# Fourier filter and gated convolution on one core: the last two blocks' convolution done block by block, the first spectral rows loaded ahead of constants, and the whole order laid out again

## The chip, the core and the metric

The kernel runs on one core of a Trainium2 chip. The metric is device time in microseconds (us). Before the change the median of three runs was 847.21 us (846.08 to 847.69). The engines are named as the profile names them: PE multiplies matrices (PEld is its weight load), DVE and ACT work element by element, POOL and SP here mostly issue transfers. Each engine executes its own instructions strictly in the order in which the program lists them.

## What is computed

```python
# x: (8, 3200, 256) float32; w_r, w_i: (256, 256); b_r, b_i: (256)
X = np.fft.rfft(x, axis=1)
Yr = Xr @ w_r - Xi @ w_i + b_r
Yi = Xr @ w_i + Xi @ w_r + b_i
Yr, Yi = soft_threshold(Yr, 0.01), soft_threshold(Yi, 0.01)   # shrink by 0.01 towards 0
y = np.fft.irfft(Yr + 1j * Yi, n=3200, axis=1)

# y then goes through a gated convolution, kernel size 5, causal, one filter per channel
gate = 1 / (1 + np.exp(-sum(conv_w[k] * y_shifted_by(4 - k) for k in range(5))))
val = y @ w_val
out = (gate * val) @ w_out
```

`w_val`, `conv_w` and `w_out` can reach the kernel as 64-bit floats; it turns them into 32-bit ones with integer operations on DVE.

## The kernel before

Eight sequences (index b) are processed in a software pipeline. A transform of length 3200 = 64 x 50 is done in two steps each way, as matrix products:

- **p1** (`p1`, unit u = 0..7): load rows of x, multiply with a 50-point transform (PE, tile `p`, L716 to L723), copy half of the result to SBUF with ACT (tile `s`, L729), form sums and differences with DVE (L736), and store to an intermediate array in device memory, `a_dram` (the stores are issued at L671 and L751, half of them by SP and half by POOL). x has 3 buffers and s has 2 for sequences 1 to 7. Sequence 0 borrows further buffers, since nothing else runs yet.
- **p2** (block d = 0..6): when all of a sequence's `a_dram` is stored, load 4 x 128 rows of it (tile `a`, issued by SP at L771, two transfers), do the second transform step (`s2`, L789), split the result into a high and a low part (ACT L830, L834, L841; DVE L837, L838, L842, tiles `sx` and `xs`), multiply with the complex weights (`mix_sum` L907 and `mix` L903, tile `y_ps`), soft-threshold (ACT L915, DVE L917, tile `tp`), do the first inverse step (`s1i`, L858) and store to `z_dram`. There are 13 units of mixing per sequence (`NU`), the unit of time of the order.
- **p3** (block k = 0..7): load from `z_dram` (tile `zl`), do the last inverse step (`positions`, L969, tile `y_p`), copy to `y_sb`. The convolution (`conv`) takes two blocks k and k+1 at a time: one ACT multiply of 800 columns for each of the two channel halves (L1017), four DVE multiply-adds of 800 columns for each half (L1020), one ACT sigmoid for each half (L1030). Then, for each block (`gated`): the product with `w_val` (tile `v_ps`), gate times value (DVE L1054), a cast and its rest (ACT L505, DVE L507) and the product with `w_out` (tile `o_ps`, L1003), a copy (L1079) and the store. The last two blocks of sequence 7 skip the cast and use plain 32-bit weights (L999).

**The order.** Every piece of work is entered with `add(at, engine, ...)`, where `at` is its due time in units of mixing. `Plan.order` is a list scheduler with a cost for each piece and modelled transfer landings. Whenever an engine is free it takes, of the pieces that could begin within 20 ns of the earliest one (50 ns on SP), the one with the lowest `at`. The result is the fixed instruction order of each engine. On the chip the engines wait for semaphores. A piece that is listed ahead of its data therefore holds up all that stands behind it on that engine. The dictionary `O` holds the offsets of `at` for each kind of piece, some of them for each sequence (`conv_6`), and a few switches: `together` and `hold` decide how readily PE pieces of the modes "q" and "h" (the small transform products) are grouped, `early_x` says for how many of sequence 0's last stores the first x loads of sequence 1 need not wait. Where PE would stand idle in the model between 4 us and 200 us, `fill` puts products with zeros (L480) there, whose result is not used.

In sequence 0 the first `a` load has `at` = 0 + `load_a` + `load_a_0` = 10.0 + 3.6 = 13.6, while the constants that also become ready when sequence 0's stores have landed have -90.4 (`load_g1`, L607, part 0) and about 0 and 4 (`load_f2`, L602, parts 1 and 2).

Of the kernel before, what the change touches and what calls it, by code (L numbers as in the profile page):

```python
# [21 lines left out]
NH = 2  # L22
# [275 lines left out]
def act(n, kind="copy"):  # L298
# [9 lines left out]
O = {'spread': -101.4442,  # L308
     'hold': 1.6848,
     'together': 1.5823,  # L310
     'later': 53.134,
     'load_x': 17.846,
     'p1': 1.5226,
     'p1_step': 1.0759,
     'load_a': 10.0019,
     's2': -2.121,
     's1i': -11.205,
     'p3': 7.122,
     'load_z': 9.4509,
     'y': 9.4717,  # L320
     'conv': 47.943,
     'val': 3.9688,
     'gate': -49.7775,
     'project': 6.045,
     'late_val': 6.023,
     'late_out': 14.484,
     'turn': -90.4451,
     'pre': -5.7976,
     'mix_sum': -1.2289,
     'p1_1': -9.8046,  # L330
     'load_x_1': -91.0314,
     'p1_2': -1.912,
     'p3_0': -0.0087,
     'cast': 0.0037,
     'cast_sum': 24.9973,
     'store': -14.2917,
     'store_1': 42.1645,
     'load_a_0': 3.5715,
     'lag': 5,
     'early_x': 4,  # L340
# [3 lines left out]
     'const': 1.7737,  # L344
     'load_x_0': 6.2588,
     'load_x_2': 11.2939,
     'load_x_3': 1.4455,
     'load_x_6': -5.698,
     'load_x_7': -13.6801,
     'store_0': 2.4949,  # L350
     'store_2': -3.9049,
     'store_3': 5.6479,
     'store_6': 7.9572,
     'store_7': -7.113,
     'load_a_1': -10.8481,
     'load_a_2': 3.8573,
     'load_a_3': -7.0617,
     'load_a_6': 3.0623,
     'load_a_7': -2.8157,
     's2_0': -0.1117,  # L360
     's2_1': 0.2815,
     's2_2': -0.0057,
     's2_3': 0.3165,
     's2_6': -0.036,
     's2_7': 0.9309,
     's1i_0': -16.6791,
     's1i_1': 0.7475,
     's1i_2': 0.3771,
     's1i_3': -9.836,
     's1i_6': -9.5474,  # L370
     's1i_7': 2.8801,
     'mix_sum_0': -0.2547,
     'mix_sum_1': -0.1504,
     'mix_sum_2': -0.9431,
     'mix_sum_3': 0.2288,
     'mix_sum_6': -0.0331,
     'mix_sum_7': 0.5012,
     'cast_0': 0.1408,
     'cast_1': 1.6748,
     'cast_2': 0.1173,  # L380
     'cast_3': -1.1395,
     'cast_6': 0.0469,
     'cast_7': 0.8641,
     'load_z_0': -2.2847,
     'load_z_1': 12.2789,
     'load_z_2': 6.4162,
     'load_z_3': 0.5923,
     'load_z_6': 9.1799,
     'load_z_7': -17.648,
     'y_0': -2.4138,  # L390
     'y_1': 7.1844,
     'y_2': -0.27,
     'y_3': 9.8876,
     'y_6': -17.7978,
     'y_7': -0.7363,
     'val_0': 0.0788,
     'val_1': 0.0095,
     'val_2': 0.5223,
     'val_3': -0.3875,
     'val_6': 1.5935,  # L400
     'val_7': -0.1154,
     'gate_0': 1.29,
     'gate_1': -6.6514,
     'gate_2': 10.3642,
     'gate_3': -13.7452,
     'gate_6': 6.0847,
     'gate_7': 5.6435,
     'project_0': -0.2308,
     'project_1': -0.2082,
     'project_2': 0.3489,  # L410
     'project_3': -0.0372,
     'project_6': 1.4085,
     'project_7': 0.8587,
     'conv_0': -12.5894,
     'conv_1': 3.8899,
     'conv_2': -5.0339,
     'conv_3': -7.0043,
     'conv_6': -5.8596,
     'conv_7': 8.2268,
     'pre_0': 6.5561,  # L420
     'pre_1': -14.0279,
     'pre_2': 4.4971,
     'pre_3': 10.0304,
     'pre_6': 2.6289,
     'pre_7': 17.1354,
     'p1_0': 24.5364,
     'p1_3': 0.2909,
     'p1_6': 0.0365,
     'p1_7': 0.0276,
     'p3_1': 0.2371,  # L430
     'p3_2': -0.3606,
     'p3_3': 0.0793,
     'p3_6': -0.8783,
     'p3_7': 0.4373}
# [9 lines left out]
def fourier_filter_then_gated_conv(ctx: ExitStack, tc: tile.TileContext, x, w_r, w_i, b_r, b_i,  # L444
# [242 lines left out]
    def p1(b, u, at):  # L687
# [64 lines left out]
        for k, (eng, queue, cost) in enumerate(QUEUES[:1] * 2 if early and u > 4 else QUEUES):  # L752
            key = ("a_dram", b, 2 * u + k)
            A_KEYS.setdefault(b, []).append(key)
            if early:
                STORED.append(("stored", 0, 2 * u + k))
            add(at + of("store", b) + 0.001 * k, eng, cost * 1.7 if u == 0 else cost, lambda k=k, queue=queue: store(k, queue), [ks + (0,), ks + (1,)],
                [key] + ([STORED[-1]] if early else []), {ka: "a_dram"} if u == k == 0 else None, kb=200, chain="a" + eng, dmas=3 if u == 0 else 2, read=False)


    def p2(b, d, at):
# [10 lines left out]
        add(at + of("load_a", b), "SP", 1330, load, A_KEYS[b], [ka + (0,)], {ka: "a"}, kb=128 * nt, chain="a", dmas=2)  # L772
# [167 lines left out]
    def y_at(k, c, tap=H0):  # L940
        return y_of(k, tap)[:, c]
# [64 lines left out]
    def conv(b, kk, at):  # L1006
# [12 lines left out]
        def tap(c, j):  # L1019
            nc.vector.scalar_tensor_tensor(out=acc(c), in0=wide(c, j), scalar=cw_sb[:, c, j:j + 1], in1=acc(c), op0=ALU.mult, op1=ALU.add)  # L1020
        for c in range(2):
# [7 lines left out]
        for c in range(2):  # L1029
            add(at + of("conv", b) + 0.15, "ACT", act(2 * TB, "sigmoid"), lambda c=c: nc.scalar.activation(  # L1030
                out=acc(c), in_=acc(c), func=AF.Sigmoid), (), [kg + (c, e) for e in range(2)])

# [166 lines left out]
```

## Time and profile before

| what | value |
|---|---|
| median of three runs | 847.21 us (846.08 to 847.69) |
| profiled execution, its own time | 845.59 us |
| its span, first to last instruction | 843.8 us |
| mean granted PE clock | 0.993 |
| PE busy / DVE busy / ACT busy / POOL busy | 825.3 / 735.9 / 596.3 / 147.9 us |
| bytes moved | 162.33 MB, mean 192 GB/s |

The 1.79 us between the profiled execution's time and its span lie around the first and the last instruction. Busy PE time includes the products with zeros. In the views that follow, a row of a timeline gives the start in us, the length in us, engine, line, operation, output and inputs, the number of instructions merged into the row, and in brackets the idle time before it with what ended it. A row of the chain gives start, length, and what held the end at that moment. In the table by windows each engine's busy time is followed by its number of instructions, then come the granted PE clock, the transfer engines' busy share and the rate.

### The profile page before, as it was taken

How to read it: one execution, taken by the hardware profiler on the slowest of the kernel's cores; microseconds unless marked ns; L12 is line 12 of the kernel's file. 1: busy time of each engine (PE TensorE's matmuls, PEld its weight loads, DVE VectorE, ACT ScalarE, POOL GpSimd, SP SyncE). 2: the span in 40 equal slices, each digit the busy share in tenths (PEclk: the TensorE clock that was granted, in tenths of full speed). 3: DMA queues.
4: the chain of work that ended last, by engine and by line, in shares of the span. 5: the costliest groups of instructions: out<-in, count | busy, mean ns of one | idle time of the engine just before them, and what ended most of it. 6: DMA issues, size and time to landing. Idle time of an engine off the chain costs nothing.

```text
span 843.8 us, 24474 instructions
## 1 busy us (share of the span) xinstructions
PE 825.3 (98%) x10036; PEld 715.3 (85%) x10036; DVE 735.9 (87%) x1006; ACT 596.3 (71%) x903; POOL 147.9 (18%) x284
## 2 busy tenths in 40 slices
PE   9999989999999999999999999999999999999997
PEld 5777768888889889898989988898888899999775
DVE  3367796989988999989988999889989899979994
ACT  2246566787877787778787777778775778777662
POOL 5332222201221121302211031301212000000000
PEclk9899999999999999999999999999999999999999
DMA  8898999867877786767966696758875455336313
GB/s 191 246 238 229 266 230 271 224 173 223 241 187 199 204 225 193 196 171 219 266 204 173 180 251 194 222 144 217 249 211 157 136 154 161 108 100 172 109 64 98
DMA packets 122665, 162.33 MB, mean 192 GB/s; under 512 B 16496, under 2 KB 102266, under 8 KB 122554
## 3 DMA queue, kind: packets, MB, share of 16 engines
q1 hardware_dynamic: 109706, 134.73, 57.1%
q0 software_dynamic: 12848, 26.04, 12.0%
q8 instruction: 80, 1.31, 0.7%
q14 instruction: 31, 0.25, 0.1%
HBM read 82.06 MB, written 78.64 MB: 190 GB/s over the span
## 4 chain that ended last, share of the span: by engine, by line
PE 75%; DVE 14%; DMA 6%; ACT 2%; issue 2%; POOL 1%; SPq 0%; DVEq 0%; ACTq 0%; POOLq 0%
PE y_ps L903 14%; PE o_ps L1003 13%; PE v_ps L1003 11%; PE y_p L969 9%; PE y_ps L907 7%; DVE acc L1020 4%; PE z_ps L858 4%; PE s L789 4%; PE p L716 4%; PE v_ps L999 3%; DMA x<-in_x 3%; DMA a_dram<-s 2%; DVE s L736 2%; PE p L480 1%; DVE xs L838 1%
## 5 line engine op out<-in xcount | busy, mean ns | idle before, releaser
L1020 DVE SCALAR_TENSOR_TENSOR acc<-y_sb,cw_sb,acc 128x800 f32<-128x800 f32 x256 | 262.4, 1044 | 31.7 <-ACT acc L1017 30.1
L903 PE MATMUL y_ps<-w_sb,xs 128*128 128x256 f32 x1152 | 153.0, 284 | 2.0 <-DVE y_ps L909 1.7
L903 PEld LDWEIGHTS y_ps<-w_sb,xs 128*128 128x128 f32 x1152 | 142.5, 189 | 12.3 <-issue 5.6
L1003 PE MATMUL o_ps<-gated,wo_sb 128*128 128x400 f32 x744 | 150.7, 350 | 0.2 <-DVE s L736 0.2
L1003 PEld LDWEIGHTS o_ps<-gated,wo_sb 128*128 128x128 f32 x744 | 133.5, 188 | 5.7 <-issue 2.3
L1003 PE MATMUL v_ps<-y_hl,wv_sb 128*128 128x400 f32 x648 | 130.0, 347 | 0.4 <-ACT y_sb L973 0.4
L671 POOL DMA_DIRECT2D x<-in_x x142 | 74.5, 530 | 295.2 <-PE p L723 286.1
L1003 PEld LDWEIGHTS v_ps<-y_hl,wv_sb 128*128 128x128 f32 x648 | 114.8, 188 | 4.0 <-ACT sx L830 0.8
L736 DVE TENSOR_TENSOR s<-p,s 128x512 f32<-128x512 f32 (+2 forms) x144 | 88.6, 624 | 28.9 <-ACT s L731 16.9
L671 POOL DMA_DIRECT2D a_dram<-s x122 | 63.9, 528 | 196.9 <-DVE s L736 166.6
L969 PE MATMUL y_p<-g_sb,zl 100*64 100x100 f32 x2048 | 96.5, 251 | 0.8 <-ACT acc L1030 0.8
L915 ACT ACTIVATE tp<-y_ps,nlam 128x512 f32<-128x512 f32 (+1 forms) x104 | 69.8, 671 | 38.5 <-PE y_ps L903 37.0
L969 PEld LDWEIGHTS y_p<-g_sb,zl 100*64 100x64 f32 x2048 | 88.9, 137 | 9.5 <-issue 4.7
L907 PEld LDWEIGHTS y_ps<-w_sb,xs 128*128 128x128 f32 x576 | 76.4, 189 | 21.3 <-issue 8.9
L907 PE MATMUL y_ps<-w_sb,xs 128*128 128x256 f32 x576 | 87.7, 289 | 5.2 <-ACT y_ps L885 2.8
L917 DVE SCALAR_TENSOR_TENSOR tp<-y_ps,tp 128x512 f32<-128x512 f32 (+1 forms) x104 | 68.4, 661 | 7.1 <-ACT tp L915 6.9
L505 ACT CAST gated<-acc 128x800 fp32r<-128x800 f32 x62 | 53.5, 863 | 27.4 <-DVE acc L1054 27.0
L729 ACT COPY s<-p 128x512 f32<-128x512 f32 x64 | 37.5, 595 | 42.4 <-PE p L723 31.6
L716 PE MATMUL p<-x,f_sb 50*64 50x512 f32 x256 | 65.5, 599 | 1.3 <-DMA x<-in_x 0.8
L723 PE MATMUL p<-x,f_sb 50*64 50x512 f32 x240 | 65.9, 601 | 0.0
L1054 DVE TENSOR_TENSOR acc<-v_ps,acc 128x800 f32<-128x800 f32 x64 | 62.8, 981 | 3.4 <-PE v_ps L999 1.7
L1079 ACT COPY o<-o_ps 128x800 f32<-128x800 f32 x63 | 51.9, 823 | 19.2 <-PE o_ps L1003 13.9
(95 smaller groups left out, 1172.0 us busy)
## 6 DMA issues: line engine op xcount, KB each, us to landing
out<-o SPq DMA_DIRECT2D x126, 200.0 KB
a<-a_dram SPq DMA_DIRECT2D x96, 256.0 KB
z_dram<-z_t SPq DMA_DIRECT2D x48, 512.0 KB
zl<-z_dram SPq DMA_DIRECT2D x64, 384.0 KB
x<-in_x SPq DMA_DIRECT2D x63, 192.0 KB
a_dram<-s POOLq DMA_DIRECT2D x61, 192.0 KB, 4.3
a_dram<-s SPq DMA_DIRECT2D x59, 192.0 KB
x<-in_x POOLq DMA_DIRECT2D x57, 192.0 KB, 5.2
```

Of the source, the lines that this page charges most:

```text
L671: eng.dma_start(out=out[lo:hi], in_=in_[lo:hi])
L716: nc.tensor.matmul(p[k * HP:(k + 1) * HP, 0, :], f1_sb[half(0), 0:HP], xt[half(0), k * 512:(k + 1) * 512], start=True, stop=True)
L723: nc.tensor.matmul(dst, f1_sb[half(1), 0:HP], back[:, 2 * k:2 * k + 2, :], start=True, stop=True)
L736: nc.vector.tensor_tensor(out=st()[lo:hi, h, n], in0=p[lo:hi, 0, n], in1=st()[lo:hi, 1, n], op=(ALU.add, ALU.subtract)[h])
L903: nc.tensor.matmul(p[:, 1 - r, :], xm(hx, c, r, i), w_sb[:, m, hw, c, :], start=False, stop=k == 5, skip_group_check=True)
L907: nc.tensor.matmul(tl[ky][:, 0], sm(hx, c, i), w_sb[:, 0, hw, c, :], start=False, stop=k == 5, skip_group_check=True)
L915: nc.scalar.activation(out=buffer(kt, "tp", [P, 2, D])[:, 0:n], in_=tl[ky][:, 0:n], func=AF.Relu, bias=nlam)
L917: add(at + 0.2, "DVE", dve(n * D), lambda: nc.vector.scalar_tensor_tensor(out=tl[kt][:, 0:n], in0=tl[ky][:, 0:n], scalar=LAM, in1=tl[kt][: ...
L969: nc.tensor.matmul(dst[e * HP:(e + 1) * HP], zt[0:Q, m, c * P + e * HP:c * P + (e + 1) * HP], g, start=True, stop=True)
L1003: nc.tensor.matmul(p[:, e, 0:TB], w[:, hw, c, e * P:(e + 1) * P], src(hy, c), start=n == 0, stop=n == 5)
L1020: nc.vector.scalar_tensor_tensor(out=acc(c), in0=wide(c, j), scalar=cw_sb[:, c, j:j + 1], in1=acc(c), op0=ALU.mult, op1=ALU.add)
L1054: add(at + of("gate", b), "DVE", dve(2 * TB), lambda: nc.vector.tensor_tensor(out=part(), in0=by_half(tl[kv][:, :, 0:TB]), in1=part(), op= ...
```

## The change

Three parts of the code change, and nearly every number of `O` with them. No arithmetic is left out or added.

1. **`conv_last`.** For sequence 7's blocks 6 and 7, `conv` hands over to a new function that works on one block (400 columns for each channel half) at a time. Where there were 2 ACT multiplies, 8 DVE multiply-adds and 2 sigmoids of 800 columns there are 4, 16 and 4 of 400. Block 7's pieces are due 19.9 units later than block 6's. By `y_keys` the rows that block 6 needs include some that come with block 7's copies, so both still wait for the last of `positions`; but block 6's sums and its gate no longer wait for block 7's multiply-adds.
2. **The first `a` load.** `load` of `p2` for b = 0, d = 0 is due at -200, ahead of all else that SP could issue when it becomes ready.
3. **Later early stores.** The planner's assumed landing of sequence 1's stores for u = 0 to 3 is 2.5 us later (`extra=2500`). This adds no instruction: it changes when the planner believes the `s` buffers and transfer lanes come free, and with that the order.
4. **The offsets.** `early_x` goes from 4 to 6, `hold` from 1.68 to 0.35, `together` from 1.58 to 1.44, and some 110 offsets move, many by 1 to 15 units. `late_val`, `late_out`, `lag`, `u_val`, `u_conv` and `u_out` stay.

```diff
-O = {'spread': -101.4442,
-     'hold': 1.6848,
-     'together': 1.5823,
-     'later': 53.134,
-     'load_x': 17.846,
+O = {'spread': -109.1423,
+     'hold': 0.3496,
+     'together': 1.4399,
+     'later': 56.8735,
+     'load_x': 22.3137,
...
-     'load_x_1': -91.0314,
+     'load_x_1': -78.2141,
...
-     'store': -14.2917,
-     'store_1': 42.1645,
-     'load_a_0': 3.5715,
+     'store': -9.2594,
+     'store_1': 48.5878,
+     'load_a_0': -4.4244,
      'lag': 5,
-     'early_x': 4,
+     'early_x': 6,
...
+     'conv_last': 19.8871,
...
             add(at + of("store", b) + 0.001 * k, eng, cost * 1.7 if u == 0 else cost, lambda k=k, queue=queue: store(k, queue), [ks + (0,), ks + (1,)],
-                [key] + ([STORED[-1]] if early else []), {ka: "a_dram"} if u == k == 0 else None, kb=200, chain="a" + eng, dmas=3 if u == 0 else 2, read=False)
+                [key] + ([STORED[-1]] if early else []), {ka: "a_dram"} if u == k == 0 else None, kb=200, chain="a" + eng, dmas=3 if u == 0 else 2, read=False, extra=2500 * (b == 1 and u < 4))
...
-        add(at + of("load_a", b), "SP", 1330, load, A_KEYS[b], [ka + (0,)], {ka: "a"}, kb=128 * nt, chain="a", dmas=2)
+        add(-200 if b == d == 0 else at + of("load_a", b), "SP", 1330, load, A_KEYS[b], [ka + (0,)], {ka: "a"}, kb=128 * nt, chain="a", dmas=2)
...
+        if (b, k) == (B - 1, NB - 2):
+            for i in range(2):
+                conv_last(b, k + i, at, kg)
+            return
...
+    def conv_last(b, k, at, kg):
+        here = y_keys(k, 1)
+        at += O["conv_last"] * (k % 2)
+
+        def acc(c):
+            if kg not in tl:
+                tl[kg] = room(kg, "acc", 4 * TB).rearrange("p (c h n) -> p c h n", c=2, h=NH)
+            return pair(tl[kg].rearrange("p c h n -> p c (h n)"), k % 2 * MB * N2, (3 - 2 * (k % 2)) * MB * N2, MB * N2)[:, c]
+        for c in range(2):
+            add(at + of("conv", b) + 0.01 * c, "ACT", act(TB, "conv"), lambda c=c: nc.scalar.mul(acc(c), y_at(k, c, 0), cw_sb[:, c, 0:1]),
+                [*here, ("cw", 0, 0)], [kg + (c, k % 2)], {kg: "acc"} if c == 0 and k % 2 == 0 else None, chain="conv")
+            for j in range(1, KC):
+                add(at + of("conv", b) + 0.02 * j, "DVE", 61 + dve(TB), lambda c=c, j=j: nc.vector.scalar_tensor_tensor(
+                    out=acc(c), in0=y_at(k, c, j), scalar=cw_sb[:, c, j:j + 1], in1=acc(c), op0=ALU.mult, op1=ALU.add),
+                    here, [kg + (c, k % 2)], delay=61 + dve(TB) + (190 if j == KC - 1 else 60))
+            add(at + of("conv", b) + 0.15, "ACT", act(TB, "sigmoid"), lambda c=c: nc.scalar.activation(out=acc(c), in_=acc(c), func=AF.Sigmoid),
+                (), [kg + (c, k % 2)])
```

More of the change, by code (lines that the diff above doesn't have):

```diff
@@ L343 @@
      'u_out': 9,
[L344 to L424, printed above, removed]
@@ new lines @@
+     'store_7': -4.7658,
+     'load_a_1': 2.0666,
+     'load_a_2': 10.7165,
+     'load_a_3': -11.8467,
+     'load_a_6': 5.9992,
+     'load_a_7': -9.9436,
+     's2_0': -0.9097,
+     's2_1': 0.75,
+     's2_2': -0.1843,
+     's2_3': 0.4292,
+     's2_6': -0.1802,
+     's2_7': 1.144,
+     's1i_0': -20.7795,
+     's1i_1': 5.5643,
+     's1i_2': 0.2323,
+     's1i_3': -8.9519,
+     's1i_6': -4.5866,
+     's1i_7': 0.4968,
+     'mix_sum_0': -3.6333,
+     'mix_sum_1': 0.4093,
+     'mix_sum_2': -4.8767,
@@ new lines @@
+     'mix_sum_3': 0.4724,
+     'mix_sum_6': -0.6844,
+     'mix_sum_7': 1.2736,
+     'cast_0': -7.9071,
+     'cast_1': 3.2096,
+     'cast_2': -12.491,
+     'cast_3': 2.4733,
+     'cast_6': -0.5755,
+     'cast_7': -16.2343,
+     'load_z_0': 8.0614,
+     'load_z_1': 7.5338,
+     'load_z_2': 7.561,
+     'load_z_3': -1.7466,
+     'load_z_6': 15.9253,
+     'load_z_7': -18.7416,
+     'y_0': -3.0115,
+     'y_1': 3.9572,
+     'y_2': -6.3024,
+     'y_3': 13.489,
+     'y_6': -18.3643,
+     'y_7': -0.838,
@@ new lines @@
+     'val_0': -0.283,
+     'val_1': 0.5984,
+     'val_2': 1.4366,
+     'val_3': 0.1304,
+     'val_6': 0.4313,
+     'val_7': 0.3005,
+     'gate_0': -1.4149,
+     'gate_1': -6.0437,
+     'gate_2': 20.0233,
+     'gate_3': -6.1785,
+     'gate_6': -5.023,
+     'gate_7': -1.0774,
+     'project_0': -0.6019,
+     'project_1': -5.0415,
+     'project_2': 0.341,
+     'project_3': -0.0785,
+     'project_6': 0.746,
+     'project_7': -0.3343,
+     'conv_0': -19.8352,
+     'conv_1': 9.7761,
@@ L435 @@
+     'conv_2': -12.6811,
+     'conv_3': -3.6892,
+     'conv_6': -20.7607,
+     'conv_7': 15.7101,
+     'pre_0': -3.6224,
+     'pre_1': -16.0697,
+     'pre_2': 14.5478,
+     'pre_3': 6.3853,
+     'pre_6': 0.1105,
+     'pre_7': 18.0907,
+     'p1_0': 27.2403,
+     'p1_3': -0.5804,
+     'p1_6': -2.7116,
+     'p1_7': 0.672,
+     'p3_1': 1.604,
+     'p3_2': 1.2734,
+     'p3_3': 1.3904,
+     'p3_6': -0.673,
+     'p3_7': 1.2073}
 WARM = 2
```

60 lines of the change are left out of this document (30 added, 30 removed).

## The prediction

> **What bounds the kernel now.** I read the page first, then a table by windows whose edges I set where PE's idle time changes its cause, then PE's products with zeros in the same windows.
>
> ```profile
> PE 825.3 (98%) x10036; PEld 715.3 (85%) x10036; DVE 735.9 (87%) x1006; ACT 596.3 (71%) x903; POOL 147.9 (18%) x284
> ```
>
> ```profile
> 0.00:40.00 40.00, 37.23 (x226) 25.66 (x226) 15.74 (x26) 10.15 (x19) 19.96 (x45) 0.91 0.88 219
> 40.00:54.00 14.00, 12.61 (x212) 9.68 (x211) 6.42 (x11) 5.07 (x9) 3.86 (x7) 1.00 1.00 238
> 54.00:97.50 43.50, 41.85 (x586) 33.15 (x586) 32.23 (x54) 27.51 (x47) 14.63 (x28) 1.00 0.87 237
> 97.50:126.70 29.20, 24.61 (x362) 19.64 (x361) 26.95 (x62) 15.54 (x28) 5.95 (x11) 0.98 0.96 245
> 126.70:839.20 712.50, 708.98 (x8656) 627.22 (x8656) 653.96 (x855) 537.60 (x803) 103.53 (x193) 1.00 0.66 186
> 839.20:843.80 4.60, 0.00 (x0) 0.00 (x0) 0.57 (x1) 0.46 (x1) 0.00 (x0) 0.81 0.34 109
> ```
>
> The columns are window, length, busy PE, PEld, DVE, ACT, POOL, then clock, transfer share, GB/s. From 126.7 to 839.2 us PE is busy for 708.98 of 712.5 us, so 3.5 us of waiting is all that an order can win there. The rows of line 480, the products with zeros (PE, PEld, clock, transfer share, GB/s), show where PE's busy time is none:
>
> ```profile
> 0.00:40.00 40.00, 20.71 (x144) 19.55 (x144) 0.91 0.88 219
> 40.00:54.00 14.00, 7.12 (x55) 6.17 (x53) 1.00 1.00 238
> 97.50:126.70 29.20, 5.71 (x44) 5.14 (x44) 0.98 0.96 245
> ```
>
> With idle time added, PE loses 20.71 + 2.77 us before 40, 7.12 + 1.39 = 8.5 us from 40 to 54, and 5.71 + 4.59 = 10.3 us from 97.5 to 126.7. Behind 126.7 PE is saturated, so a piece of work that starts earlier in these holes shortens the whole run by as much, provided that nothing later runs dry instead. Transfers are the resource that could: their share is 0.87 to 1.00 in all four early windows. The last 4.6 us are the final copies and the landing of the last store; no part of the change touches them.
>
> **The first a load.** SP's timeline, and SP's own waits:
>
> ```profile
> 34.33 2.30 SPq L671 DMA_DIRECT2D x<-in_x  x6
> 37.05 0.36 SPq L607 DMA_DIRECT2D g_sb<-in_g  x1
> 37.46 0.87 SPq L602 DMA_DIRECT2D f_sb<-in_f  x1
> 38.76 3.03 SPq L771 DMA_DIRECT2D a<-a_dram  x4
> ```
>
> ```profile
> SPq L607 <- DMA a_dram<-s: 0.4, 1, 0.4
> ```
>
> At 37.05 SP had waited 0.4 us for sequence 0's last store, which is also all that the a load waits for. It then issued the constants g (part 0) and f, and the a load came at 38.76. With due time -200 it goes at 37.05: 38.76 - 37.05 = 1.7 us earlier. The second a load of that row still stands behind the constants and stays where it is, about two issues after them, which is in time: it feeds the second block only. Nothing misses the constants: g is first read behind the mixing that begins at 53 us (below), and the part of f concerned serves the second block.
>
> Both sides of this price are open. At best the load is issued where the x loads are now, at 34.33, which would be 4.4 us. At worst `early_x` 6 in place of 4 puts the three x loads of SP ahead of the last stores, and the a load waits for those stores:
>
> ```profile
> x<-in_x SPq DMA_DIRECT2D x63, 192.0 KB
> ```
>
> The six issues are three of 192 KB and three small ones, at least 576 KB, and at the window's 238 GB/s they take 2.5 us, a loss if the a load stands still behind them. I take -1.7: the x bytes are ahead of the a load in both orders, only the constants change sides.
>
> **Later early stores.** What stands between the first block's data and PE's first mixing? PE, then ACT, then DVE, then the chain of waits:
>
> ```profile
> 46.38 1.16 PE L789 MATMUL s<-f_sb,a 64*64 64x64 f32 x64
> ...
> 53.02 0.51 PE L907 MATMUL y_ps<-w_sb,xs 128*128 128x256 f32 x2 [1.09 <-ACT xs L841]
> 53.83 0.74 PE L907 MATMUL y_ps<-w_sb,xs 128*128 128x256 f32 x4 [0.30 <-DVE xs L842]
> ```
>
> ```profile
> 48.09 1.02 ACT L834 CAST xs<-s 128x1024 fp32r<-128x1024 f32 x1
> 51.87 0.58 ACT L729 COPY s<-p 128x512 f32<-128x512 f32 x1 [2.75 <-DMA a_dram<-s]
> 52.35 0.62 ACT L841 CAST xs<-sx 128x512 fp32r<-128x512 f32 x1
> ```
>
> ```profile
> 49.15 0.69 DVE L837 TENSOR_TENSOR sx<-s,sx 128x512 f32<-128x512 f32 x1 [3.21 <-ACT xs L834]
> 49.75 1.21 DVE L838 TENSOR_TENSOR xs<-s,xs 128x1024 fp32r<-128x1024 f32 x1
> ...
> 53.09 0.68 DVE L842 TENSOR_TENSOR xs<-sx,xs 128x512 fp32r<-128x512 f32 x1
> ```
>
> ```profile
> 45.97 5.59 DMA a_dram<-s
> ```
>
> ACT's copy L729 for sequence 1 waits for a buffer that a store frees, and that store took 5.59 us. Behind it on ACT stands the cast L841, whose input was complete at 49.15 + 0.69 = 49.84. Behind that cast wait DVE's L842 and PE's L907. The planner had believed in an earlier landing. With 2.5 us added to it, L729 goes behind the cast. Then L841 ends at 49.84 + 0.62 = 50.46, L842 follows L838 (49.75 + 1.21 = 50.96) and ends at 51.64, and L907's low part starts at about 51.7 instead of 53.83: -2.1 us. The bound on the gain is ACT's whole idle time, 2.75 us. On the other side a later L729 can push a p1 unit out of the hole into the saturated stretch, which costs what one unit takes on PE:
>
> ```profile
> 42.82 0.58 PE p L716 x2
> 43.41 0.42 PE p L716 x2
> ```
>
> That is 0.58 + 0.42 = 1.0 us. I take -2.1. It adds to the first term, because the waiting store depends on sequence 1's rows and not on the a load.
>
> **Block by block at the end.**
>
> ```profile
> L1020 DVE SCALAR_TENSOR_TENSOR acc<-y_sb,cw_sb,acc 128x800 f32<-128x800 f32 x36 | 36.4, 1043 | 0.4 <-ACT acc L1017 0.2
> ```
>
> ```profile
> L1073 DVE COPY o<-o_ps 128x400 f32<-128x400 f32 x1 | 0.6, 575 | 5.0 <-ACT o L1073 5.0
> ```
>
> ```profile
> 831.54 0.99 DVE L1054 TENSOR_TENSOR acc<-v_ps,acc 128x800 f32<-128x800 f32 x1 [0.94 <-ACT acc L1030]
> 833.75 0.99 DVE L1054 TENSOR_TENSOR acc<-v_ps,acc 128x800 f32<-128x800 f32 x1 [1.21 <-PE v_ps L999]
> ```
>
> Eight multiply-adds of 1.043 us become sixteen of 400 columns, which the trace does not show. The lower bound is half, 0.52 us (no change in sum). The upper one is the 400-column copy, 0.575: 16 x 0.575 - 8 x 1.043 = +0.9 us. I take +0.5 on DVE and 0 on the end. PE runs without a gap until 839.1, and the idle 0.94 + 1.21 us in front of the last two gates covers it. Uncovered it would cost its 0.5. There is no gain either, since PE's work is the same and PE ends the run.
>
> [...]
>
> **The rest of the order.** The offsets change the places of thousands of instructions, without a row that shows the new ones. Between 126.7 and 839.2 at most 3.5 us are there to win. What there is to lose is the grouping of PE's modes, told under the rivals. I take 0.
>
> **Sum.** -1.7 - 2.1 + 0 + 0 = -3.8 us. The profiled execution took 845.59 us (span 843.8 and 1.8 around it) and would take 841.8. It lies 1.6 us under the median, so the median goes from 847.2 to **843.4**. The runs before spread by about 0.2% (1.7 us), so less than that counts as no change.
>
> **The rivals.** First, **the second hole shrinks too**: re-laid offsets for sequence 1's loads and the weight conversion recover half of the 10.3 us between 97.5 and 126.7, and the median is 843.4 - 5.1 = 838.3. For it speaks a wait like the one below; against it DVE's 26.95 busy us of 29.2 and a transfer share of 0.96 there:
>
> ```profile
> 124.30 2.15 PE L907 MATMUL y_ps<-w_sb,xs 128*128 128x256 f32 x12 [2.80 <-ACT y_ps L885]
> ```
>
> Second, **the gain is given back at the transfers**: sequence 1's rows must be in before its second step, they arrive no sooner at a share of 0.96, and the hole at 97.5 grows by what the first one lost: 847.2. Against it, 0.87 in the window before leaves 0.13 x 43.5 = 5.7 us of free transfer time.
>
> Third, **slower, by split groups on PE**. The chain of waits near the end shows the price:
>
> ```profile
> 755.69 1.52 PE y_p L969 x32
> 757.22 2.38 PE v_ps L1003 x12
> 759.60 2.17 PE o_ps L1003 x12
> 761.77 2.18 PE v_ps L1003 x12
> 763.95 2.90 PE y_p L969 x64
> ```
>
> Two y_p groups apart take 2 x 1.52 us, together 2.90, which is 0.14 less; and the first v_ps behind a group takes 2.38 in place of 2.18, 0.20 more. Each extra excursion into the small products costs 0.34 us. `hold` falls from 1.68 to 0.35, so a lone piece is put off less. The kernel has 64 y_p groups, and as many again of other small products. Eleven more excursions use up the 3.8 us, and from 16 on (5.4 us) the change is slower than what can be told. With 19 (6.5 us) the median is 849.9. Against it, `together`, which joins pieces that are both ready, hardly moves.
>
> **How the numbers follow.** 0.42 for the forecast (own range 841 to 845.5), 0.20 for the second hole, 0.20 for the transfers (845.5 to 849), 0.18 for split groups. Faster by over 0.2%: 0.41 + 0.20 = 0.61. Slower: 0.18. The same: 0.21. The range from 838.3 to 849.5 takes in the first two rivals' centres and most of the third; below it lie the best ends of both terms together.
>
> **What would show it.** Right: the load L771 directly behind the last store's landing; ACT's L841 ahead of the L729 that waits for a store; PE's first L907 before 50 us; DVE's sixteen short multiply-adds without a PE gap after 820; PE still at 99% from there to the end. Wrong: the first L907 at 53 or later; a hole at 97 to 127 larger than 10.3 us; or PE's busy time without zeros, 825.3 - 34 = 791 us now, larger by more than 2 us, which would be the split groups.

## The result, and the profile after

The changed kernel takes **856.73 us** (853.66 to 858.3, four runs). The kernel before took 847.45 us beside it (846.08 to 849.15). The ratio is 1.0116, 95% interval [1.0093, 1.0139]: 9.3 us slower, where the prediction had 3.8 us faster and a range up to 849.5. The profiled execution of after is the slowest of its four, 858.3 us (span 856.2), with the lowest mean clock of the four (0.984; the others 0.986 to 0.988), so its profile shows 12.4 us more span than the profile of before. The accounts below are of these 12.4 us; the runs' medians say that a usual execution loses some 3 us less.

Lines of code behind the edits have moved by one: the x product L716 is now L717, the a load L772, the second transform step L790, the mixing products L904 and L908, the products with zeros L481. The sixteen short multiply-adds are L1050.

The page's engine row, and the window table with PE, PEld, DVE, ACT, POOL, clock, transfer share and GB/s:

```profile
PE 829.3 (97%) x10002; PEld 715.0 (84%) x10002; DVE 740.4 (86%) x1014; ACT 596.6 (70%) x907; POOL 148.5 (17%) x284
```

```profile
0.00:40.00 40.00, 36.74 (x224) 24.84 (x224) 15.72 (x26) 10.16 (x19) 20.02 (x45) 0.91 0.86 213
40.00:54.00 14.00, 10.63 (x132) 7.59 (x128) 4.47 (x8) 2.20 (x5) 5.97 (x11) 0.88 0.79 187
54.00:97.50 43.50, 40.19 (x611) 33.42 (x611) 29.96 (x46) 26.97 (x44) 10.61 (x21) 0.96 0.84 224
97.50:126.70 29.20, 23.98 (x300) 19.74 (x299) 24.27 (x57) 14.77 (x27) 6.87 (x13) 0.88 0.93 250
126.70:140.00 13.30, 10.17 (x117) 7.28 (x119) 10.79 (x19) 5.34 (x9) 4.20 (x8) 0.74 0.69 207
140.00:851.50 711.50, 707.58 (x8636) 622.17 (x8628) 654.65 (x859) 536.71 (x804) 100.82 (x187) 1.00 0.64 184
```

The same windows for the products with zeros alone (PE, PEld, clock, transfer share, GB/s):

```profile
0.00:40.00 40.00, 20.02 (x132) 18.67 (x132) 0.91 0.86 213
40.00:54.00 14.00, 5.34 (x39) 4.77 (x40) 0.88 0.79 187
54.00:97.50 43.50, 4.49 (x22) 4.11 (x21) 0.96 0.84 224
97.50:126.70 29.20, 2.33 (x18) 2.25 (x18) 0.88 0.93 250
```

Two rows of before that the prediction did not need, the first of its zeros, the second of all its work:

```profile
54.00:97.50 43.50, 0.60 (x4) 0.53 (x4) 1.00 0.87 237
...
126.70:140.00 13.30, 13.30 (x212) 10.67 (x212) 8.49 (x15) 8.76 (x16) 3.25 (x7) 0.93 0.96 283
```

PE's loss in a window is its idle time and its zeros together:

| window, us | loss before | loss after | difference |
|---|---|---|---|
| 0 to 40 | 23.5 | 23.3 | -0.2 |
| 40 to 54 | 8.5 | 8.7 | +0.2 |
| 54 to 97.5 | 2.3 | 7.8 | +5.5 |
| 97.5 to 140 | 10.3 | 10.7 | +0.4 |
| 140 to the end | 8.1 | 8.6 | +0.5 |

That is 6.4 us. The other 6.0 are PE's useful work (busy time without zeros), which went from 791.1 to 797.1 us, although the matrix work is the same. The clock column says where to look: it is 0.74 to 0.96 in four windows in which it was 0.93 to 1.00 before. A count of the products supports this. Behind 140 us after has more of them still to do than before (64 more L970, 12 more each of L904 and L908, and others), and PE is busy there for 707.6 us instead of 695.7. Priced at before's busy time for each kind, the additional products make up 10.8 of these 11.9 us. So by this estimate some 1 us of the 6.0 was lost behind 140 us and some 5 us ahead of it. Nearly all of the loss thus lies ahead of 140 us, and the end is the forecast one.

**The first hole did not shrink, it moved on by 6 us.** SP, then PE, ACT and DVE around the first block:

```profile
33.69 2.68 SPq L672 DMA_DIRECT2D x<-in_x  x6
36.48 1.67 SPq L672 DMA_DIRECT2D a_dram<-s  x4
40.35 0.64 SPq L672 DMA_DIRECT2D x<-in_x  x2
42.66 0.63 SPq L672 DMA_DIRECT2D a_dram<-s  x2
43.82 0.71 SPq L752 DMA_DIRECT2D a_dram<-s  x1
44.76 1.35 SPq L772 DMA_DIRECT2D a<-a_dram  x2
```

```profile
51.80 1.97 PE L790 MATMUL s<-f_sb,a 64*64 64x64 f32 x60 [2.95 <-DMA a<-a_dram]
53.70 4.08 PE L481 MATMUL y_ps<-zero_sb 128*128 128x128 f32 x18
57.71 1.16 PE L790 MATMUL s<-f_sb,a 64*64 64x64 f32 x64
...
59.27 1.66 PE L908 MATMUL y_ps<-w_sb,xs 128*128 128x256 f32 x12
```

```profile
53.82 1.01 ACT L835 CAST xs<-s 128x1024 fp32r<-128x1024 f32 x1 [4.34 <-DMA a<-a_dram]
54.73 0.59 ACT L831 COPY sx<-s 128x512 f32<-128x512 f32 x1
```

The a load goes ahead of the constants, as the edit says. But `early_x` 6 has put the six x issues before sequence 0's last four store issues on SP, and in SP's fixed order an x load (two issues) and three store issues of sequence 1 have come to stand between the last of those and the a load. The load goes at 44.76, where before it went at 38.76. PE's first mixing product starts at 59.27 instead of 53.02. The casts have changed sides too: xs now stands before sx, and the sum, which the first L908 needs, comes last.

**The second hole is as long as before, but more of it is idle time and less of it zeros.** The PE rows with the longest waits, each with a later row of the same shape:

```profile
110.10 2.93 PE L904 MATMUL y_ps<-w_sb,xs 128*128 128x256 f32 x12 [3.09 <-DVE y_ps L910]
...
132.31 1.42 PE L908 MATMUL y_ps<-w_sb,xs 128*128 128x256 f32 x6 [3.13 <-ACT y_ps L886]
...
135.71 2.93 PE L904 MATMUL y_ps<-w_sb,xs 128*128 128x256 f32 x12
...
146.67 0.98 PE L908 MATMUL y_ps<-w_sb,xs 128*128 128x256 f32 x6
147.49 1.57 PE L904 MATMUL y_ps<-w_sb,xs 128*128 128x256 f32 x12
```

What L910 had been behind, on DVE, is the conversion of a weight:

```profile
102.80 2.15 DVE L548 TENSOR_SCALAR st<-st 128x512 int32<-128x512 int32 x5
...
109.61 0.43 DVE L910 TENSOR_TENSOR y_ps<-y_ps,bias_sb 128x256 f32<-128x256 f32 x1
```

Thirteen steps without a gap take 109.61 - 102.80 = 6.8 us. They stand in the kernel before too; there 3.39 us of zeros covered much of the first block. Behind each idle time of 3 us the same products take longer: twelve L904 2.93 us against 1.57, nearly twice as long, and six L908 1.42 against 0.98. From these rows, two groups of L904 lose 2.7 us, L908 0.4 and the sixty products at 51.80 some 0.9 (64 of them take 1.16 at 57.71). That is 4.0 us, without the other products of the same stretches, such as those between 133.7 and 135.7. Before had one such place, the 2.80 us wait at 124.30 that the prediction quotes, where twelve L907 took 2.15. So by my estimate the lower clock is at least about half of the 6.0 us.

### The profile page after: what moved, and what is told of

Read it like the earlier page. It is cut to its first block, busy times and chain, and to the rows that moved or that the text cites. A ratio compares the mean times of both kernels' runs of the same rounds, so it can differ in the third digit from the quotient of the medians.

```text
span 856.2 us, 24404 instructions
## 1 busy us (share of the span) xinstructions
PE 829.3 (97%) x10002; PEld 715.0 (84%) x10002; DVE 740.4 (86%) x1014; ACT 596.6 (70%) x907; POOL 148.5 (17%) x284
## 4 chain that ended last, share of the span: by engine, by line
PE 83%; DVE 9%; ACT 3%; DMA 2%; issue 2%; POOL 0%; SPq 0%; DVEq 0%; ACTq 0%; POOLq 0%
PE o_ps L1004 15%; PE y_ps L904 14%; PE v_ps L1004 12%; PE y_p L970 10%; PE y_ps L908 8%; PE z_ps L859 5%; PE p L717 5%; PE s L790 5%; PE v_ps L1000 3%; DVE acc L1021 3%; PE p L481 2%; DVE s L737 2%; DMA a_dram<-s 1%; DVE st L548 1%; PE p L724 1%
## 5 line engine op out<-in xcount | busy, mean ns | idle before, releaser
L1021 DVE SCALAR_TENSOR_TENSOR acc<-y_sb,cw_sb,acc 128x800 f32<-128x800 f32 x248 | 255.3, 1057 | 14.8 <-ACT acc L1018 13.9
L904 PEld LDWEIGHTS y_ps<-w_sb,xs 128*128 128x128 f32 x1152 | 144.1, 191 | 18.0 <-DVE y_ps L910 6.4
L904 PE MATMUL y_ps<-w_sb,xs 128*128 128x256 f32 x1152 | 154.3, 285 | 4.3 <-DVE y_ps L910 4.3
L970 PE MATMUL y_p<-g_sb,zl 100*64 100x100 f32 x2048 | 96.9, 251 | 0.7 <-DVE acc L1077 0.7
L970 PEld LDWEIGHTS y_p<-g_sb,zl 100*64 100x64 f32 x2048 | 89.0, 137 | 9.7 <-issue 3.8
L908 PEld LDWEIGHTS y_ps<-w_sb,xs 128*128 128x128 f32 x576 | 75.7, 190 | 20.0 <-issue 6.4
L908 PE MATMUL y_ps<-w_sb,xs 128*128 128x256 f32 x576 | 87.8, 291 | 4.5 <-ACT y_ps L886 4.5
L839 DVE TENSOR_TENSOR xs<-s,xs 128x1024 fp32r<-128x1024 f32 x48 | 58.4, 1219 | 13.6 <-ACT sx L831 8.8
L790 PEld LDWEIGHTS s<-f_sb,a 64*64 64x64 f32 x3072 | 53.2, 136 | 18.6 <-issue 7.8
L717 PE MATMUL p<-x,f_sb 50*64 50x512 f32 x256 | 66.7, 611 | 1.1 <-ACT z_t L866 0.8
L724 PE MATMUL p<-x,f_sb 50*64 50x512 f32 x240 | 66.9, 612 | 0.1
```

The source lines that it names most:

```text
L717: nc.tensor.matmul(p[k * HP:(k + 1) * HP, 0, :], f1_sb[half(0), 0:HP], xt[half(0), k * 512:(k + 1) * 512], start=True, stop=True)
L724: nc.tensor.matmul(dst, f1_sb[half(1), 0:HP], back[:, 2 * k:2 * k + 2, :], start=True, stop=True)
L790: nc.tensor.matmul(p[e * HP:(e + 1) * HP, h, c, t, :], tl[ka][rows, t, c * P + e * HP:c * P + (e + 1) * HP], f2_sb[rows, (4 * d + t) * N1: ...
L904: nc.tensor.matmul(p[:, 1 - r, :], xm(hx, c, r, i), w_sb[:, m, hw, c, :], start=False, stop=k == 5, skip_group_check=True)
L908: nc.tensor.matmul(tl[ky][:, 0], sm(hx, c, i), w_sb[:, 0, hw, c, :], start=False, stop=k == 5, skip_group_check=True)
L970: nc.tensor.matmul(dst[e * HP:(e + 1) * HP], zt[0:Q, m, c * P + e * HP:c * P + (e + 1) * HP], g, start=True, stop=True)
```

## The experiments

All times are medians; the ratio is to the kernel before on the same chip, with its 95% interval. Some of the kernels move single pieces of the **finished order** and leave everything else where it was. In these the products with zeros also stay as they were, so a wait that such a product covers can't be won back in them. In the others the planner lays the order out anew, as the change itself does. An excursion, in the table, is a change of PE from its products with the weights to the small transform products.

| kernel | what it is | us | ratio |
|---|---|---|---|
| x1_load | before, finished order, a load ahead of constants | 846.25 | 0.9997 [0.9979, 1.0014] |
| x2_cast | before, finished order, casts ahead of waiting copy | 845.68 | 0.9989 [0.9973, 1.0005] |
| e3_conv | before, convolution edit alone | 846.42 | 0.9991 [0.9976, 1.0005] |
| e1_load | before, load edit alone, laid out anew | 854.71 | 1.0090 [1.0065, 1.0116] |
| e2_extra | before, later early stores alone, laid out anew | 870.90 | 1.0289 [1.0268, 1.0311] |
| e5_edits | all three edits, old offsets | 859.82 | 1.0159 [1.0141, 1.0178] |
| e4_offsets | new offsets, no edit | 878.09 | 1.0357 [1.0329, 1.0385] |
| x5_split | before, 30 more excursions | 860.62 | 1.0163 [1.0138, 1.0189] |
| j_before, j_after | before and after, seven excursions fewer | 850.47, 860.44 | 1.0054 [1.0033, 1.0076], 1.0162 [1.0138, 1.0187] |
| x3_after | after, a load behind the last store | 854.73 | 1.0101 [1.0077, 1.0125] |
| a_first | after, first hole rearranged | 853.27 | 1.0078 [1.0051, 1.0104] |
| a_conv, b_conv | after and before, pieces moved out from behind the conversions | 856.71, 850.85 | 1.0120 [1.0097, 1.0144], 1.0056 [1.0037, 1.0075] |
| a_both | a_first with a_conv | 854.99 | 1.0098 [1.0076, 1.0119] |
| a_spread, b_spread | after and before, conversions spread out | 852.64, 850.27 | 1.0067 [1.0049, 1.0085], 1.0041 [1.0026, 1.0055] |
| a_firstspread | a_first with a_spread | 852.73 | 1.0069 [1.0048, 1.0090] |

**The two terms of the sum, each alone on the finished order.** x1_load and x2_cast move what the terms spoke of, and nothing else.

```diff
 x1_load:  done = self.order()
+        self.place(done, "SP", [("a", (0, 0))], "before", ("SP", [("g1", 0)]), new=True)
 x2_cast:  done = self.order()
+        self.place(done, "ACT", [("s1", (1, 2))], "behind", ("ACT", [("xs", (0, 0)), ("sx", (0, 0))]), new=True)
+        self.place(done, "DVE", [("s1", (1, 2))], "behind", ("DVE", [("xs", (0, 0)), ("sx", (0, 0))]))
```

> The order of the kernel before, unchanged but for one piece: sequence 0's first a load stands ahead of the two constants on SP. The prediction's first term: the load goes 1.7 us earlier and so does the end, -1.7 us against before (845.7). Rival: PE's first mixing waits for ACT, and ACT for a store of sequence 1 that lands at 51.6 us whatever the load does, so the 1.7 us stop there: 0 within 0.8 us.

> The order of the kernel before, unchanged but for two pieces: ACT's copy L729 of sequence 1's unit 2, which waits for a store to land, stands behind the cast L841 of the first block, and DVE's first sum of that unit behind L842. The prediction's second term: PE's first mixing begins 2.1 us earlier and the end comes 2.1 us earlier (845.3). Rival: PE's next piece, p1 of unit 3, needs the bank that this copy frees, so PE stops there until the same store has landed: the first L907 is earlier, the p1 behind it is not, and the end moves by less than 0.8 us.

Measured: no change in either. x1_load's load goes at 37.13, as the term said. PE's rows there (the line numbers of x1_load and x2_cast are a few higher):

```profile
44.87 1.83 PE L490 MATMUL y_ps<-zero_sb 128*128 128x128 f32 x14
46.63 1.16 PE L799 MATMUL s<-f_sb,a 64*64 64x64 f32 x64
```

The second step starts without a wait behind zeros, at 46.63 (46.38 before): in this order PE was not waiting for the load, since zeros and x products stand ahead. In x2_cast the casts do come forward. The gain is limited at first by zeros that stay in the order, and then dissolves in the next waits:

```profile
50.22 2.05 PE L491 MATMUL y_ps<-zero_sb 128*128 128x128 f32 x16
52.03 0.93 PE L918 MATMUL y_ps<-w_sb,xs 128*128 128x256 f32 x6
...
55.74 3.16 PE L914 MATMUL y_ps<-w_sb,xs 128*128 128x256 f32 x24 [0.88 <-DVE y_ps L920]
...
59.51 1.16 PE L800 MATMUL s<-f_sb,a 64*64 64x64 f32 x64 [0.16 <-DMA f_sb<-in_f]
```

The kernel before, at the second and third of these places (the first, at 53.02, is in the prediction):

```profile
56.33 2.99 PE L903 MATMUL y_ps<-w_sb,xs 128*128 128x256 f32 x24
...
59.69 1.16 PE L789 MATMUL s<-f_sb,a 64*64 64x64 f32 x64
```

x2_cast is 1.0 us earlier at the first place, 0.6 at the second and 0.2 at the third: a DVE add, and then a constant's load, are late next. Both moves together, with fewer zeros in these places, were not run; the prediction's sum assumed that their gains add.

**The parts alone, laid out anew.** e1_load and e2_extra take one edit each, e3_conv the convolution, e5_edits all three with the old offsets, e4_offsets the offsets without an edit (with `conv_last` unused). The diffs are the lines of the change itself.

> The kernel before with the block by block convolution of the last two blocks alone, offsets as before (and 19.9 units for block 7). The order of PE is unchanged. The prediction's term: 0 within 0.8 us, DVE's added half us lying in the idle time in front of the last two gates. Rival: DVE, busy for 19.2 of 20 us there, is late for the last products and the end is 1 to 3 us later.

> The kernel before with only one line of the change: the first a load takes its place in the list by -200, ahead of the constants, and the order is laid out anew with the old offsets. As predicted for this part: 1.7 us less, about 845. Rival (x1_load: PE does not wait for this load, but for its own work ahead of it and for ACT): 846 to 847.5; its order leaves PE's products for small ones 96 times, the kernel before 95 times, so a new order costs nothing by the excursions.

> The kernel before with only one line of the change: the 2500 ns later end that the list is told for sequence 1's first four store pairs (with the old offsets; the order is laid out anew). As predicted for this part: 2.1 us less, 845. Rival (a new order moves work everywhere, and this one leaves PE's products for small ones 111 times where the kernel before does it 95 times): 3 to 8 us more, 850 to 855.

> All three code edits with the offsets of the kernel before: no offset moved, but the assumed later landings lay the whole order out anew. SP issues the first a load ahead of the constants and with no store of sequence 1 ahead of it. PE changes 109 times into the small products, 95 before. Theory: 14 times 0.48 us is +6.7 and the early hole gives nothing back, 853. Rival (the edits as such are good and only the moved offsets cost): 843 to 846.

> The kernel before, none of the three edits, with all the changed offsets. As predicted (the rest of the order is worth nothing): 846 to 848. Rival (the offsets belong to the edits; this order leaves the products for small ones 115 times, 20 more than the kernel before, at 0.31 us of PE time and up to 0.48 us in all for each, and keeps early_x at 6): 6 to 12 us more, 853 to 859.

Only the convolution does what was expected; PE's order is the same in e3_conv. The same load edit that is worth nothing on the finished order costs 7.9 us once the order is laid out anew, although there the first block does gain. SP's row and PE's in e1_load:

```profile
37.29 1.86 SPq L772 DMA_DIRECT2D a<-a_dram  x2
```

```profile
50.64 1.68 PE L908 MATMUL y_ps<-w_sb,xs 128*128 128x256 f32 x12
```

The load directly follows the x loads, and the first mixing product starts 2.4 us earlier than in the kernel before (50.27 in e5_edits). All of that and more is lost later. The later stores cost 24 us, the offsets without their edits 31. PE's profiled span, taken apart (zeros are the sum of the page's zero rows, useful is busy less zeros, idle is span less busy):

| kernel | span | useful | zeros | idle |
|---|---|---|---|---|
| before | 843.8 | 791.1 | 34.2 | 18.5 |
| after | 856.2 | 797.1 | 32.2 | 26.9 |
| e1_load | 852.7 | 792.3 | 42.8 | 17.6 |
| e5_edits | 858.0 | 794.9 | 44.1 | 19.0 |
| e2_extra | 869.3 | 797.6 | 44.9 | 26.8 |
| e4_offsets | 876.2 | 804.3 | 34.7 | 37.2 |
| x5_split | 857.8 | 800.3 | 34.2 | 23.3 |
| a_spread | 849.2 | 793.6 | 30.5 | 25.1 |
| a_firstspread | 852.4 | 797.6 | 30.9 | 23.9 |

In e1_load nearly the whole loss is zeros, 8.6 us more of them, in these two groups above all:

```profile
92.58 4.63 PE L481 MATMUL p<-zero_sb 128*128 128x128 f32 x40
114.78 8.30 PE L481 MATMUL y_ps<-zero_sb 128*128 128x128 f32 x72
```

They are put where the list expects PE to have nothing to do, and the second group lies over DVE's second block of conversion steps:

```profile
113.35 2.14 DVE L548 TENSOR_SCALAR st<-st 128x512 int32<-128x512 int32 x5
```

With the new offsets there are fewer zeros and more idle time (after against e5_edits in the table); beside the edits the offsets recover about 3 us (859.8 to 856.7), without them they cost 31.

**What an excursion costs.** x5_split lets PE leave its products with the weights for the small ones 30 times more often; the j kernels put short runs of products with the weights behind the next small group, which removes seven excursions.

```diff
 x5_split:  done = self.order()
+        self.split(done, 30)
 j_before, j_after:  done = self.order()
+        self.join(done, 60, 120000, 2)
```

> The order of the kernel before, but at 30 places one product with the weights is put between two transform steps that stood side by side on PE: 30 more changes into the small products, 125 instead of 95. The price of the prediction's third rival, 0.34 us each: +10.2 us (857.6). If the 0.34 us is hidden behind weight loads or lies in the waits only: 0 to +3 us. In the changed kernel there are 106 such changes, 11 more than before, so the outcome says how much of its loss they can be: 3.7 us at 0.34.

> The order of the kernel before, but at 7 places past the first 120 us a short run of products with the weights, standing alone between two groups of transform steps on PE, is put behind the second group: 88 changes into the small products instead of 95. At the 0.48 us that the splitting run showed for each (14.3 us for 30): -3.3 us, 843.0, below both kernels. If the price holds only for added ones, because here others wait for the products that were put back: 0 within 1 us.

> The order of the changed kernel with the same treatment: 99 changes into the small products instead of 106. Theory (split groups are a good part of its loss): -3.3 us against the changed kernel, 853.4. Rival (its loss lies in the first 140 us alone): 856.7 within 1 us.

x5_split is 14.3 us slower, 0.48 for each excursion: 0.31 of useful PE time (800.3 - 791.1 = 9.2 us over 30) and the rest in idle time. The prediction's 0.34 is right for PE's own part. Taking excursions out gave nothing back: both j kernels are 3 to 4 us slower. Their useful time did not fall (791.7 and 798.3 us), and their idle time grew by 3.9 and 3.7 us, so the products that were put back made others wait. After has 106 excursions, before 95. Eleven at 0.31 us would be 3.4 us. In a_spread, whose mean clock is about that of before (0.992 and 0.993), useful time is 2.5 us above before. The count of products behind 140 us leaves less for them: 1.1 us in after and 2.1 in a_spread. So by my estimate the excursions are 1 to 2.5 us of the loss.

**The first hole.** x3_after moves only the a load, to where the edit was meant to put it. a_first also puts SP's last two stores of sequence 0 back ahead of the x loads, and sx ahead of xs; in its diff, the piece with the first number goes directly behind that with the second.

```diff
 x3_after:  done = self.order()
+        self.place(done, "SP", [("a", (0, 0))], "before", ("SP", [("x", (1, 3))]), new=True)
 a_first:  done = self.order()
+        for n, m in (69, 62), (70, 69), (123, 107), (126, 125), (128, 111):
+            self.behind(done, n, m)
```

> The order of the changed kernel, but sequence 0's first a load stands on SP directly behind sequence 0's last store, ahead of an x load and three stores of sequence 1 that wait for PE and DVE. Theory: the in-order queue of SP held the load; it goes when the last store has landed, about 41 us instead of 44.8, PE's first mixing begins 3 to 4 us earlier than in the changed kernel, and the median is 3 to 4 us below it (853). Rival: the load's long landing (6.3 us) is what counts, bytes ahead of it on the same rings: then the first mixing and the end stay (856.7, within 1.5 us).

> The changed kernel's own finished order, with five pieces moved around its first hole and nothing else: sequence 0's last four stores (two of them SP's) again stand before the next sequence's x loads, the first a load follows directly behind the three SP x loads, and the cast sx of the first block stands before xs on ACT and on DVE. Theory (the first hole is a real part of the loss): with the a load alone moved, x3_after came 2.0 us below the changed kernel; with its x loads out of the way and the sum path's casts first, the first L908 comes before 54 us instead of at 59.27 and the time falls by 3 to 5 us against the 856.7 of the changed kernel, to about 853. Rival (what stands behind this hole takes the gain): no more than the 2.0 of x3_after, 854.7 or above.

x3_after is 2.0 us below after, too little for the intervals to tell it from no change. Its load goes at 39.64, 5.1 us earlier than in after, but its first mixing product only 2.0 us earlier (57.23), since PE now waits 3.03 us for rows of x at 45.87. a_first is 3.5 us below after. In it the first mixing product starts at 53.76 instead of 59.27, 5.5 us earlier, and part of that is lost again ten microseconds later:

```profile
53.76 1.78 PE L926 MATMUL y_ps<-w_sb,xs 128*128 128x256 f32 x12
...
62.91 1.98 PE L808 MATMUL s<-f_sb,a 64*64 64x64 f32 x64 [3.23 <-issue]
```

So the first hole is likely a part of the loss, and the 3.5 us lie within the theory's 3 to 5. The time alone does not show it, because the interval of a_first (up to 1.0104) still meets that of after (from 1.0093).

**The conversions.** a_conv, a_both and b_conv move five pieces (six in b_conv), the adds that PE needs and the copies of the bias into y_ps by ACT (the seeds), out from behind the conversion steps. a_spread, a_firstspread and b_spread let the steps alternate with DVE's other work; w_out's staging takes other buffers for that.

```diff
 a_conv:  done = self.order()
+        for n, m in (346, 345), (343, 342), (576, 575), (582, 581), (603, 582):
+            self.behind(done, n, m)
 a_spread:  done = self.order()
+        self.spread(done, list(range(257, 270)), 0, 2, [270, 271])
+        self.spread(done, list(range(313, 326)), 4, 2, [326, 327])
...
+        tags = ("acc", "acc", "o") if name == "w_out" else ("zl", "zl", "zl")
```

> The changed kernel's own finished order, with five pieces moved out from behind the two blocks of 13 conversion steps and nothing else: the adds of y_ps and tp, and the seeding of y_ps on ACT, stand directly behind what each needs. Theory (the second hole is a real part of the loss): the 3.09 us before L904 at 110.10 and the 3.13 us before L908 at 132.31 go, and with them the granted clock of 0.72 and 0.66 in the 10 us behind each, worth about 4 us more by the lengths of the same matmuls: 5 to 8 us less than the 856.7 of the changed kernel, about 850.5. Rival (the next wait takes over, as in x2_cast): at most 1.5 us less, 855.2 or above.

> Both sets of moves on the changed kernel's order. Theory (the loss is two holes with the clock behind them, plus a smaller part from more small-product excursions, about 3 us, that stays): the two gains add, 8 to 12 us less than 856.7, about 847 to 849. Rival (both holes are covered by what follows them, the excursions are the loss): under 3 us less, 853.7 or above.

> The kernel before, its own finished order, with the same adds and seeds moved out from behind the conversion steps (six pieces). Theory: the 2.80 us before PE's work at 124.30 and the clock of 0.83 in 120 to 130 us, about 1.8 us, are worth up to 4 us: about 843 to 845 beside 847. Rival (the weights' conversion itself, or the next add, becomes late instead): no change, 846 to 848.

> The changed kernel's own finished order; the 26 conversion steps of the two weights alternate with the DVE work that follows them (two other pieces ahead of each step) instead of standing in two blocks of 6.7 us, and w_out's staging takes the accumulators' and the outputs' buffers, free until then, so that its steps may run past the first z loads. No step is left out. Theory (the second hole and its clock are DVE's two blocks, whichever piece stands behind them): the 3.09 us and the 3.13 us go without the 4.70 and the 3.45 us that took their place in a_conv, and the granted clock stays at 1: 6 to 9 us less than 856.7, about 849.5. Rival (the DVE work is late wherever it stands): 855 or above.

> The same together with a_first's five moves. Theory (all of the loss lies before 140 us, in idle PE time and the clock behind it): 9 to 12 us less than 856.7, so 845 to 848, no slower than the kernel before by more than 0.2%. Rival (the excursions of the new order cost 0.31 us or more each over the whole run): it stays 3 to 5 us above the kernel before, 850 or above.

> The same spreading on the kernel before's own finished order. Theory: the 2.80 us before L907 at 124.30 and about 1.8 us of low clock go, with nothing as large in their place (unlike b_conv, where 5.4 us of wait arose before one L903 group): 842 to 845. Rival (its zeros and its order cover the blocks already, and the steps delay others): 846 or above.

The two waits of 3 us go in a_conv, and the time stays. Other work is now behind the same steps:

```profile
109.21 0.58 PE L912 MATMUL y_ps<-w_sb,xs 128*128 128x256 f32 x1 [3.45 <-ACT y_ps L904]
...
131.56 1.12 PE L735 MATMUL p<-x,f_sb 50*64 50x512 f32 x2 [4.70 <-DVE s L755]
```

a_both, at 855.0 us, gains no more than x3_after, as its rival said. b_conv did the same to the kernel before and made it 4.7 us slower, with one wait of 5.38 us before L921. Only dissolving the blocks helps clearly: a_spread is 4.1 us below after, a little under half of the loss. Its interval does not meet that of after, but the gain is less than the 6 to 9 us expected. Its longest wait between 97 and 140 us, on PE:

```profile
126.92 0.98 PE L949 MATMUL y_ps<-w_sb,xs 128*128 128x256 f32 x6 [2.39 <-ACT y_ps L927]
```

Both cures together (a_firstspread) give no more than one, 852.7 us. b_spread is slower than before by 3.6 us: the 2.80 us wait is gone from it, but there is one of 2.75 us before the zeros at 110.91 and one of 1.51 us at 126.51. No version of either kernel was faster than the kernel before by more than the noise.

## Why the prediction was wrong

**The first a load, -1.7.** The step took the wait for granted: the load "at 38.76" to "37.05". On the finished order it moved just so and was worth 0 (x1_load), because the second step's start is set there by PE's own order, zeros included, and the casts by ACT. And in the changed kernel the load is not earlier but 6.0 us later, at 44.76. The bound named `early_x` 6, the x loads ahead of the last stores, and priced it by transfer bytes, at 2.5 us. What was missed is the order on SP's queue: the list lets the load in only once the stores that it needs are placed, and by then it has put an x load and three stores that wait for PE and DVE ahead of it. The due time of -200 decides only among work that is ready. With the old offsets the same edit does put the load directly behind the x loads (37.29 in e1_load), so it is the new offsets that hold it back; which of them besides `early_x` is not shown.

**Later early stores, -2.1.** The mechanism was right: moved behind the cast, the copy no longer holds it, and the first mixing product starts 1.0 us earlier. The price was wrong: it counted a gain at one point of the chain as a gain of the run. Sixteen zeros that end just ahead of the first mixing product left 1.0 of the 2.1 us, and this was down to 0.2 after 7.5 us more. As a line of the planner's input it costs 24 us alone.

**The convolution, 0.** Right (e3_conv: -0.1%). DVE's rows in before, then in after:

```profile
820.12 2.00 DVE L1020 SCALAR_TENSOR_TENSOR acc<-y_sb,cw_sb,acc 128x800 f32<-128x800 f32 x2
```

```profile
834.85 1.72 DVE L1050 SCALAR_TENSOR_TENSOR acc<-y_sb,cw_sb,acc 128x400 f32<-128x400 f32 x3
...
841.72 3.90 DVE L1050 SCALAR_TENSOR_TENSOR acc<-y_sb,cw_sb,acc 128x400 f32<-128x400 f32 x7
```

One multiply-add of 400 columns takes 0.629 us in the trace, but in a row the next one starts before the last has ended, so three take 1.72. The sixteen keep DVE busy for about 9.1 us (three groups of three and one of seven), the eight of 800 columns for 8.0 (four groups of two). That is about 1 us more, where +0.5 was taken within a bound of +0.9. The bound was too low because it let one short multiply-add take no longer than a copy, 0.575 us. PE runs into the end without a gap (busy for 19.00 of the 19 us from 832 to 851), so the extra was covered.

**The rest of the order, 0.** This is the step that failed. The sum priced each edit as a move of its own piece with all else in place, and put at 0 whatever the planner moves along with it, without a row that showed the new order. With the old offsets the three edits cost 12.6 us where the sum had 3.8 us of gain (e5_edits); beside them the new offsets take about 3 us of this back. The four orders laid out anew with other places for PE's work cost 7.9 us (e1_load), 12.6 (e5_edits), 24 (e2_extra) and 31 (e4_offsets), and these do not add up, so no part has a price of its own. The prediction said that behind 126.7 us at most 3.5 us were there to win, which no run contradicts, and that what could be lost was the grouping of PE's modes. In after the loss is nearly all elsewhere, ahead of 140 us: the first mixing 6.2 us later, part of the second hole's zeros turned into idle time, and the lower clock around the idle times.

**The rivals.** The second hole did not shrink: up to 126.7 us it fell from 10.3 to 7.6, but 3.1 us of it moved on to behind that point. The transfers did not take the gain: their share fell in every early window (0.86, 0.79, 0.84 and 0.93 up to 126.7 us, where before had 0.88, 1.00, 0.87 and 0.96). The split groups had the right price (0.31 measured, 0.34 worked out) and the right direction, but there were only eleven more of them, 1 to 2.5 us of 9.3 by my estimate; the forecast of that case, 849.9, was right in sign alone. Two of the prediction's own signs of being wrong came: "the first L907 at 53 or later" (59.27), and useful PE time grew by more than 2 us, by my estimate more by the clock than by groups.

**What stays open.** With the first hole closed and the conversions dissolved, a_firstspread still lies 6 us above before. In its profile (854.2 us) useful PE time is 6.5 and idle time 5.4 us above before, zeros 3.3 below. The count of products behind 140 us leaves 1.9 us of the 6.5 there, about as much as in a_spread (2.1). So by this estimate some 4.6 us arose ahead of 140 us, where few of the excursions are and where the clock was lower than in a_spread (0.96 from 54 to 97.5 us and 0.92 from 97.5 to 140, against 0.99 and 0.96). Why idle time and low clock stay when both holes are treated, and so why the two cures do not add, these runs do not show.

## What to carry to other kernels

On an engine that is saturated from some point on, an edit that removes a wait upstream is worth what is left of the gain when the saturated stretch begins (in x2_cast 1.0 us was down to 0.2 after 7.5 us); follow it through the next three waits before putting it into a sum. Price an edit to a planner's input by laying the order out and counting idle time, filler and mode changes in it, not by the one wait that it was meant for. In after the a load stood behind three stores in SP's order and went at 44.76; placed ahead of them, in x3_after, it went at 39.64. So an earlier due time is worth nothing until what stands ahead is also named.

## What the runs showed of the hardware

In after, PE's granted clock fell to 0.50 in or just behind each of three idle times of PE (2.95, 3.09 and 3.13 us), and stayed there for some 6.8 us each time. Windows around the second of them, with the same columns as above:

```profile
107.00:110.00 3.00, 0.01 (x2) 0.00 (x0) 2.87 (x7) 0.97 (x2) 0.00 (x0) 0.79 1.12 238
110.00:112.00 2.00, 1.90 (x9) 1.90 (x10) 1.97 (x5) 0.61 (x2) 0.00 (x0) 0.50 1.13 230
112.00:114.00 2.00, 2.00 (x11) 2.00 (x11) 1.79 (x9) 0.69 (x1) 1.45 (x3) 0.50 1.01 295
114.00:116.00 2.00, 2.00 (x40) 1.78 (x43) 1.66 (x7) 0.37 (x1) 0.35 (x1) 0.61 0.51 146
...
118.00:120.00 2.00, 0.48 (x12) 0.02 (x4) 1.72 (x2) 2.00 (x5) 1.52 (x3) 1.00 0.84 253
120.00:122.00 2.00, 1.75 (x13) 1.68 (x14) 1.83 (x3) 1.61 (x4) 0.00 (x0) 1.00 1.08 266
```

An idle time of 3.09 us, which ends at 110.10, is followed by some 5 us at 0.50. The mean of 0.79 from 107 to 110 says that the clock fell before the idle time ended. In the kernel before, the clock fell behind the 2.80 us that end at 124.30 and was at 0.50 for some 3.4 us. The idle time of 1.77 us that ends at 120.25 leaves the clock at 1.00 in the last two rows. In these runs the length of a wait did not decide alone. In a_spread a wait of 2.39 us left the clock as it was (six products in 0.98 us, shown above); in a_firstspread the same wait before the same products did not:

```profile
128.49 1.15 PE L951 MATMUL y_ps<-w_sb,xs 128*128 128x256 f32 x6 [2.39 <-ACT y_ps L929]
```

From the clock columns (window times missing share, doubled, since the low clock is 0.50) the low stretch from 97.5 to 126.7 us in after lasted about 0.12 x 29.2 x 2 = 7.0 us and the one from 126.7 to 140 about 0.26 x 13.3 x 2 = 6.9. Of these, 5.4 and 6.8 us lie behind the end of the idle time, so by my estimate, half of that, the two idle times of some 3 us cost about 3 us more each behind them. Behind the 3.39 us of zeros at 99.55 in the kernel before, the clock stayed at 1.00 (99 to 104 us) and 64 products L789 take 1.16 us, as they do elsewhere, so these zeros cost their own time alone. That is why a hole of unchanged length became dearer.
